# Softmax exponentials without a bias operand: the common factor moved into VectorE's exponent constant

## The chip, the cores and the metric

The kernel runs on one core of a Trainium2 chip. The metric is the device time of one execution in microseconds; lower is better. Every timed kernel was run four times (one of them profiled), next to runs of the kernel before on the same chip; the last experiment was run once.

## The reference, cut to what matters

```python
xn = layernorm(A_x)                                  # [1, 2048, 512]
out = A_x + attention(xn, wqkv, wo) + token_mlp(xn, w1, b1, w2, b2)

def attention(x, wqkv, wo):                          # 32 heads of 16
    q, k, v = split(x @ wqkv)
    p = softmax(q @ k.T * 16 ** -0.5, axis=-1)       # 32 x 2048 x 2048 exponentials
    return merge_heads(p @ v) @ wo
# [the MLP: layernorm, w1 + b1, gelu (tanh form), w2 + b2]
```

There are 134 million exponentials, and the softmax divides by their sum. A factor common to all exponentials of one row therefore cancels; it only has to be the same in numerator and denominator.

## The kernel before

The attention goes through 32 blocks of 32 score tiles. A tile is 128 keys by 1024 columns and fills two PSUM banks; three such slots take turns (`n % 3`). Of the 32 tiles of a block (all blocks but the first), 26 go to ScalarE's `Exp` and six to VectorE, which builds an exponential from integer operations on the bits of a bfloat16: `W` is a first guess, `A` its power of two, `M` a product that corrects the mantissa; TensorE adds up the three.

```python
KAPPA = 2.16705
LNKAPPA = 0.773366911
CM = 171.0 / 1024.0
IBIAS = 16256.0                      # 127 * 128: the exponent bias of bfloat16
DPOS = (2, 7, 12, 17, 22, 27)        # the VectorE tiles of a block of 32
LAG, LAGD = 2, 4                     # periods from scores to the matmuls with V
# ...
kap = sb("kap", [128, 1], F32)
sc.add("pool", lambda e: e.memset(kap[:], LNKAPPA), writes=[("kap",)])
# ...
def pslot(n):
    return n % 2 if n < 2 * NKT else n % 3

def exp_act(n):
    # [buffer bookkeeping cut]
    sc.add("act", lambda e: e.activation(pT[:, buf, :], ps[:, s_ * 1024:(s_ + 1) * 1024], ACTF.Exp,
                                         bias=kap[:], scale=LN2_128),
           reads=[("bank", 2 * s_), ("bank", 2 * s_ + 1), ("kap",)], writes=[("pT", buf)], name="exp")

def exp_dve(n):
    # [buffer bookkeeping cut]
    sc.add("dve", lambda e: e.tensor_scalar(dW_i[:, buf, :], ps[:, s_ * 1024:(s_ + 1) * 1024], IBIAS, 0.0,
                                            ALU.add, ALU.max), ...)              # frees the PSUM slot
    sc.add("dve", lambda e: e.tensor_scalar(dm1_i[:], dW_i[:, buf, :], 0x7f, 0x3f80,
                                            ALU.bitwise_and, ALU.bitwise_or), ...)
    yield                                                                        # next period
    sc.add("dve", lambda e: e.tensor_scalar(dA_i[:, buf, :], dW_i[:, buf, :], -128, None, ALU.bitwise_and), ...)
    sc.add("dve", lambda e: e.tensor_tensor(dm1[:], dm1[:], dm1[:], ALU.mult), ...)
    yield                                                                        # next period
    sc.add("dve", lambda e: e.tensor_tensor(dM[:, buf, :], dW[:, buf, :], dm1[:], ALU.mult), ...)

# the order of the matmuls with V, in pv_seq:
steps.append([g + LAG, [(n, "P") for n in ns]])          # ScalarE tiles
steps.append([g + LAGD, [(n, "W")]])                     # VectorE tiles: three pairs of matmuls
steps.append([g + LAGD, [(n, "A")]])
steps.append([g + LAGD, [(n, "M")]])
```

VectorE's three terms add up to KAPPA times the exponential. So that ScalarE's tiles carry the same factor, their exponentials get the bias ln(KAPPA), which is a pointer to a column of 128 values. A period is one group of two score tiles; TensorE's program runs period by period: the scores of a period, then matmuls with V of earlier periods, then a piece of projections or of the MLP.

The softmax here doesn't subtract the row's maximum and nothing guards it: scores larger than these inputs give would overflow.

## Time and profile before

| | before |
|---|---|
| time, median of 3 (lowest to highest) | 948.09 us (945.67 to 950.41) |
| ScalarE busy | 868.3 us, 91% |
| TensorE busy | 806.3 us, 85% |
| VectorE busy | 778.2 us, 82% |

The engines' busy times, from the first part of the page (engine, busy us, share of the span, instructions):

```profile
PE 806.3 (85%) x5752; PEld 237.4 (25%) x5828; DVE 778.2 (82%) x1296; ACT 868.3 (91%) x859; POOL 35.5 (4%) x78
```

Groups of instructions, from the page (line, engine, operation, output and inputs, shape, count | busy us, mean ns of one | idle us of the engine before them, and what ended most of it):

```profile
L828 ACT ACTIVATE pT<-ps,kap 128x1024 bf16<-128x1024 f32 x838 | 857.6, 1138 | 57.9 <-PE ps L805 55.1
L805 PE MATMUL ps<-QT,KT 32*128 32x512 bf16 x2048 | 328.6, 409 | 104.7 <-ACT pT L828 69.1
L837 DVE TENSOR_SCALAR dW<-ps 128x1024 int16<-128x1024 f32 x186 | 227.0, 1221 | 106.7 <-PE ps L805 105.4
```

838 instructions of 1138 ns would be 954 us, but they are busy for only 857.6: neighbours overlap. So the duration of one is not what it costs. What it costs is the distance from one start to the next when nothing else holds the engine up. ScalarE's timeline shows it (start us, length us, engine, line, operation, count):

```profile
193.83 2.14 ACT L828 ACTIVATE pT<-ps,kap 128x1024 bf16<-128x1024 f32 x2
195.82 0.66 ACT L669 ACTIVATE ga_sb<-ga_sb 128x512 f32<-128x512 f32 x1
196.34 3.16 ACT L828 ACTIVATE pT<-ps,kap 128x1024 bf16<-128x1024 f32 x3
```

Two exponentials take from 193.83 to 195.82, about 996 ns each; the Tanh of the GELU behind them takes 0.52 us until the next start.

Three waits (waits view; who waited for what: us in total, times, longest):

```profile
PE ps L805 <- ACT pT L828: 69.1, 168, 1.6
ACT pT L828 <- PE ps L805: 55.1, 85, 2.2
PE ps L805 <- DVE dW L837: 29.4, 42, 2.7
```

The chain that ended last, by engine and by line:

```profile
ACT 43%; PE 34%; DVE 20%; issue 2%; DMA 1%; SPq 0%; ACTq 0%; POOL 0%; DVEq 0%
```

### The profile page before, as it was taken

How to read it: one execution, taken by the hardware profiler on the slowest of the kernel's cores; microseconds unless marked ns; L12 is line 12 of the kernel's file. 1: busy time of each engine (PE TensorE's matmuls, PEld its weight loads, DVE VectorE, ACT ScalarE, POOL GpSimd, SP SyncE). 2: the span in 40 equal slices, each digit the busy share in tenths (PEclk: the TensorE clock that was granted, in tenths of full speed). 3: DMA queues.
4: the chain of work that ended last, by engine and by line, in shares of the span. 5: the costliest groups of instructions: out<-in, count | busy, mean ns of one | idle time of the engine just before them, and what ended most of it. 6: DMA issues, size and time to landing. Idle time of an engine off the chain costs nothing.

```text
span 949.7 us, 14370 instructions
## 1 busy us (share of the span) xinstructions
PE 806.3 (85%) x5752; PEld 237.4 (25%) x5828; DVE 778.2 (82%) x1296; ACT 868.3 (91%) x859; POOL 35.5 (4%) x78
## 2 busy tenths in 40 slices
PE   5888898988788888888889888998988889788885
PEld 3423233322222222222222222222222222222221
DVE  6688989877788878788888888887888778787787
ACT  5998999998889989899999899998999999999995
POOL 5402000000000000000000000000000000000000
PEclk9989999987888989799999999998999889878898
DMA  5020000011111111111110111100100000000000
GB/s 156 1 51 5 27 6 8 8 29 24 28 29 29 29 23 30 23 21 31 23 42 24 22 37 37 26 20 22 37 22 7 7 7 18 12 7 8 7 8 22
DMA packets 71411, 23.08 MB, mean 24 GB/s; under 512 B 63216, under 2 KB 69360, under 8 KB 71344
## 3 DMA queue, kind: packets, MB, share of 16 engines
q1 hardware_dynamic: 68176, 20.59, 9.8%
q10 hardware_dynamic: 3168, 1.57, 0.6%
q8 instruction: 45, 0.74, 0.3%
q14 instruction: 22, 0.18, 0.1%
HBM read 19.54 MB, written 2.35 MB: 23 GB/s over the span
## 4 chain that ended last, share of the span: by engine, by line
ACT 43%; PE 34%; DVE 20%; issue 2%; DMA 1%; SPq 0%; ACTq 0%; POOL 0%; DVEq 0%
ACT pT L828 42%; PE ps L853 15%; PE ps L805 11%; DVE dW L837 7%; PE ps L654 3%; PE ps L681 2%; DVE dM L849 2%; DVE dm L846 1%; DVE QT L479 1%; DVE dm L840 1%; PE ps L466 1%; DVE KT L456 1%; PE ps L618 1%; DVE u_sb L659 1%; DVE ga_sb L662 1%
## 5 line engine op out<-in xcount | busy, mean ns | idle before, releaser
L828 ACT ACTIVATE pT<-ps,kap 128x1024 bf16<-128x1024 f32 x838 | 857.6, 1138 | 57.9 <-PE ps L805 55.1
L805 PE MATMUL ps<-QT,KT 32*128 32x512 bf16 x2048 | 328.6, 409 | 104.7 <-ACT pT L828 69.1
L837 DVE TENSOR_SCALAR dW<-ps 128x1024 int16<-128x1024 f32 x186 | 227.0, 1221 | 106.7 <-PE ps L805 105.4
L853 PE MATMUL ps<-pT,V 128*32 128x512 bf16 x1676 | 255.8, 416 | 5.8 <-DVE OT L738 4.3
L805 PEld LDWEIGHTS ps<-QT,KT 32*128 32x128 bf16 x2048 | 80.5, 91 | 391.6 <-ACT pT L828 235.3
L849 DVE TENSOR_TENSOR dM<-dW,dm 128x1024 bf16<-128x1024 bf16 x186 | 128.0, 688 | 4.2
L846 DVE TENSOR_TENSOR dm<-dm 128x1024 bf16<-128x1024 bf16 x186 | 127.2, 684 | 0.0
L853 PEld LDWEIGHTS ps<-pT,V 128*32 128x32 bf16 x1676 | 62.6, 97 | 115.8 <-issue 82.1
L840 DVE TENSOR_SCALAR dm<-dW 128x1024 int16<-128x1024 int16 x186 | 80.4, 432 | 6.4
L853 PE MATMUL ps<-dM,VM 128*32 128x512 bf16 x372 | 79.0, 421 | 0.0
L853 PE MATMUL ps<-dW,V 128*32 128x512 bf16 x372 | 78.6, 419 | 0.0
L853 PE MATMUL ps<-dA,V 128*32 128x512 bf16 x372 | 78.2, 417 | 0.0
L844 DVE TENSOR_SCALAR dA<-dW 128x1024 int16<-128x1024 int16 x186 | 76.2, 410 | 0.0
L654 PE MATMUL ps<-big,w1blk 128*128 128x512 bf16 (+1 forms) x156 | 53.0, 413 | 4.0 <-issue 4.0
L681 PE MATMUL ps<-gT,w1blk 128*128 128x512 bf16 (+1 forms) x157 | 51.4, 391 | 3.0 <-issue 3.0
L701 PE MATMUL ps<-wo_pad,oT 128*128 128x512 bf16 x105 | 32.9, 383 | 2.4 <-issue 2.4
L853 PEld LDWEIGHTS ps<-dW,V 128*32 128x32 bf16 x372 | 18.1, 94 | 46.4 <-issue 46.4
L853 PEld LDWEIGHTS ps<-dM,VM 128*32 128x32 bf16 x372 | 20.2, 105 | 25.1 <-issue 6.4
L738 DVE COPY OT<-ps 128x512 f32<-128x512 f32 x31 | 21.3, 688 | 5.7 <-PE ps L853 4.1
L479 DVE TENSOR_SCALAR QT<-ps,qmask 128x512 bf16<-128x512 f32 x30 | 21.1, 744 | 5.3 <-PE ps L466 5.2
L760 DVE TENSOR_TENSOR oT<-OT,denb 128x512 bf16<-128x512 f32 x31 | 21.2, 684 | 0.0
L456 DVE CAST KT<-ps 128x128 bf16<-128x128 f32 (+1 forms) x26 | 12.3, 472 | 9.5 <-PE ps L430 6.3
(74 smaller groups left out, 324.8 us busy)
## 6 DMA issues: line engine op xcount, KB each, us to landing
w1blk<-in_B_w_dram SPq DMA_DIRECT2D x10, 512.0 KB, 4.2
w1blk<-in_B_w_dram SPq DMA_DIRECT2D x16, 320.0 KB, 3.3
denb<-rden_scratch SPq DMA_DIRECT2D x124, 32.0 KB, 1.8
out_dram<-osb SPq DMA_DIRECT2D x16, 128.0 KB, 1.7
dcomp<-OT SPq DMA_DIRECT2D x124, 2.0 KB, 1.7
x_sb<-in_A_x_dram SPq DMA_DIRECT2D x3, 512.0 KB, 9.4
wqkv_sb<-in_A_wqkv_dram ACTq DMA_DIRECT2D x3, 384.0 KB, 11.0
wo_pad<-in_A_wo_dram SPq DMA_DIRECT2D x8, 64.0 KB, 2.0
```

What stands on the lines that cost most here:

```text
L479: sc.add("dve", lambda e, e_=e_, slot=slot: e.tensor_scalar(QT[:, slot, :], bank(bk), qmask[:, e_:e_ + 1], None, ALU.mult), reads=[("bank" ...
L654: sc.add("pe", lambda e, st=st: e.matmul(bank(EX_BANK)[0:m, :], lhsT=w1blk[:, slot, st, 0:m], rhs=h_sb[:, st, :], start=(st == 0), stop=(s ...
L681: sc.add("pe", lambda e, ft=ft, m=m: e.matmul(bank(EX_BANK), lhsT=w2blk[0:m, slot, ft, :], rhs=gT[0:m, ft, :], start=(ft == 0), stop=(ft = ...
L701: sc.add("pe", lambda e, G=G: e.matmul(bank(EX_BANK), lhsT=oT[:, par, G, 128 * sti:128 * (sti + 1)], rhs=wo_pad[:, G, :], start=(G == 0), ...
L805: sc.add("pe", lambda e, r=r, bk=bk: e.matmul(bank(bk), lhsT=KT[32 * r:32 * r + 32, T, 128 * kt:128 * (kt + 1)], rhs=QT[32 * r:32 * r + 32 ...
L828: sc.add("act", lambda e: e.activation(pT[:, buf, :], ps[:, s_ * 1024:(s_ + 1) * 1024], ACTF.Exp, bias=kap[:], scale=LN2_128), reads=[("ba ...
L837: sc.add("dve", lambda e: e.tensor_scalar(dW_i[:, buf, :], ps[:, s_ * 1024:(s_ + 1) * 1024], IBIAS, 0.0, ALU.add, ALU.max), reads=[("bank" ...
L840: sc.add("dve", lambda e: e.tensor_scalar(dm1_i[:], dW_i[:, buf, :], 0x7f, 0x3f80, ALU.bitwise_and, ALU.bitwise_or), reads=[("dW", buf)], ...
L844: sc.add("dve", lambda e: e.tensor_scalar(dA_i[:, buf, :], dW_i[:, buf, :], -128, None, ALU.bitwise_and), reads=[("dW", buf)], writes=[("d ...
L846: sc.add("dve", lambda e: e.tensor_tensor(dm1[:], dm1[:], dm1[:], ALU.mult), reads=[("dm1",)], writes=[("dm1",)], name="dm2")
L849: sc.add("dve", lambda e: e.tensor_tensor(dM[:, buf, :], dW[:, buf, :], dm1[:], ALU.mult), reads=[("dW", buf), ("dm1",)], writes=[("dM", b ...
L853: sc.add("pe", lambda e: e.matmul(bank(PV_BANK)[32 * r:32 * r + 32, :], lhsT=lhs, rhs=rhs, start=first, stop=last, tile_position=(0, 32 * r)),
```

## The change

Instead of bringing ScalarE's exponentials up to KAPPA, VectorE's are brought down: its exponent constant becomes 127·128 − 128·log2(KAPPA), a number that is not an integer. The factor is gone from all tiles, and ScalarE's bias falls back to an immediate zero.

```diff
-LNKAPPA = 0.773366911
-CM = 171.0 / 1024.0
-IBIAS = 16256.0
+IBIAS = 127.0 * 128.0 - 128.0 * float(np.log2(KAPPA))      # CM only moves up
@@
-        kap = sb("kap", [128, 1], F32)
@@
-        sc.add("pool", lambda e: e.memset(kap[:], LNKAPPA), writes=[("kap",)])
@@ exp_act
-                                                 bias=kap[:], scale=LN2_128),
-                   reads=[("bank", 2 * s_), ("bank", 2 * s_ + 1), ("kap",)], writes=[("pT", buf)], name="exp")
+                                                 scale=LN2_128),
+                   reads=[("bank", 2 * s_), ("bank", 2 * s_ + 1)], writes=[("pT", buf)], name="exp")
```

More of the change, by code (lines that the diff above doesn't have):

```diff
@@ L36 @@
 LN2_128 = 0.6931471805599453 / 128.0
+CM = 171.0 / 1024.0
 KAPPA = 2.16705
-LNKAPPA = 0.773366911
-CM = 171.0 / 1024.0
-IBIAS = 16256.0
+IBIAS = 127.0 * 128.0 - 128.0 * float(np.log2(KAPPA))
 DPOS = (2, 7, 12, 17, 22, 27)
```

## The prediction

> **What bounds the kernel now.** Chiefly ScalarE's softmax exponentials. The page's engine table has ScalarE busy 868 us of the 949.7 us span (91%), TensorE 806 (85%), VectorE 778 (82%). The groups table has 838 exponentials of 128x1024 occupying 857.6 us, with only 57.9 us idle before them, nearly all waiting for the score matmuls. The chain of waits runs 42% through them. No engine is far behind: over the 32 blocks of attention ScalarE needs about 27 us a block, VectorE about 25, TensorE about 25, and a block lasts about 28.8 us ((937 - 15)/32, from the timeline). VectorE's share is 186 tiles of 1221 + 432 + 410 + 684 + 688 = 3435 ns (groups), 20 us a block, plus about 4 us of other work.
>
> **What the change does.** The order of instructions is the same on every engine, apart from one small memset at the start that goes away on GpSimd. VectorE's and TensorE's instructions stay the same in number and shape; one VectorE constant is no longer an integer. The only cost that can change is ScalarE's: the 838 exponentials lose their per-partition bias operand; the built program then carries an immediate zero.
>
> **What that is worth each.** From the timeline: back to back, exponentials start every 996 ns, though one lasts 1113 ns or more (they overlap). 1024 elements at the 0.833 ns of the Trainium skill ("ScalarE: Activation LUTs", section "What ACT_TABLE_LOAD costs") are 853 ns, so 143 ns of a period are fixed. The same section says that a pointer operand adds about 93 ns to one activation; the trace agrees: at 512 elements the query copy with a scale pointer took 687 ns, the transposed copies without one 597. But part of this is overlapped. Where the Tanh (no pointer, 512 elements = 427 ns) was issued back to back, the next started 519 ns after it: 92 ns fixed. So I expect the period to fall by about 51 ns, 996 to 945, not by 93; the duration of one should fall by about 90, 1138 to about 1045.
>
> **On the critical path.** 838 x 51 ns = 43 us of ScalarE work. About 82% of ScalarE's instructions start back to back; there the gain counts in full at first. But VectorE, at 25 us a block, then is as long as ScalarE (about 25), and TensorE close behind, also with throttled stretches (granted clock 0.81 from 200 to 300 us, where ScalarE is busy only 84%). Score matmuls already wait 29 us for VectorE's evictions of score tiles (waits view); these waits should grow. I count on 55 to 70% of the 43 us: about 26 us.
>
> **Prediction: 922 us, range 907 to 936 (8 in 10). Faster by over 2% 0.72, within 2% 0.27, slower 0.01.**
>
> **What would show the steps.** (1) Mean duration of an exponential about 1045 ns; spacing back to back about 945 ns in the timeline. (2) ScalarE busy about 825 us. (3) VectorE and TensorE busy within 10 us of 778 and 806, so higher shares. (4) ScalarE's idle time before exponentials up from 58 us by 10 to 25 us, with score matmuls waiting longer for VectorE's evictions and less for ScalarE. (5) The result stays correct.
>
> **What would make it wrong.** The pointer's cost may be wholly hidden in the overlap of neighbours: then the period stays 996 and the time about 948. It may be not hidden at all: period near 905, ScalarE gains 76 us, and the time falls to 895 to 910 with VectorE and TensorE as limits. Exponentials read PSUM and the Tanh SBUF, so the 92 ns may not carry over. [...]

## The result, and the profile after

The changed kernel took 907.27 us (median of 4, 901.64 to 911.73) against 948.39 us (median of 4). The ratio is 0.9565, with a 95% interval of 0.9494 to 0.9636. Here and below, a ratio is the mean time of one kernel's fast runs over that of the other's of the same rounds, so it is not quite the ratio of the medians quoted. The result is correct.

The engines' busy times, and the groups, from the page of after:

```profile
PE 790.7 (87%) x5828; PEld 232.9 (26%) x5828; DVE 775.4 (85%) x1296; ACT 801.4 (88%) x859; POOL 35.5 (4%) x77
```

```profile
L825 ACT ACTIVATE pT<-ps 128x1024 bf16<-128x1024 f32 x838 | 790.6, 1045 | 82.8 <-PE ps L802 79.5
L802 PE MATMUL ps<-QT,KT 32*128 32x512 bf16 x2048 | 312.9, 403 | 91.6 <-ACT pT L825 44.2
L834 DVE TENSOR_SCALAR dW<-ps 128x1024 int16<-128x1024 f32 x186 | 227.1, 1221 | 77.8 <-PE ps L802 77.5
```

The duration of an exponential fell from 1138 to 1045 ns, by 93. VectorE's eviction is unchanged at 1221 ns. TensorE's busy time reads 16 us lower although its instructions are the same (76 matmul records are missing from the trace of before, so that the true fall is larger); its mean granted clock was 0.942 after and 0.920 before. No experiment tells why.

ScalarE's timeline, again around a Tanh behind exponentials:

```profile
189.66 1.98 ACT L825 ACTIVATE pT<-ps 128x1024 bf16<-128x1024 f32 x2
191.46 0.68 ACT L666 ACTIVATE ga_sb<-ga_sb 128x512 f32<-128x512 f32 x1
191.98 5.66 ACT L825 ACTIVATE pT<-ps 128x1024 bf16<-128x1024 f32 x6
```

Two exponentials now take from 189.66 to 191.46: by the starts in the trace 903 ns each, 93 less than the 996 of before. The Tanh, which never had a pointer, still takes 0.52 us.

The waits and the chain:

```profile
ACT pT L825 <- PE ps L802: 79.5, 150, 2.3
PE ps L802 <- ACT pT L825: 44.2, 134, 1.8
PE ps L802 <- DVE dW L834: 40.8, 53, 3.0
```

```profile
PE 42%; DVE 29%; ACT 24%; DMA 2%; issue 2%; SPq 1%; DVEq 0%; ACTq 0%; POOL 0%
```

So the whole saving on ScalarE is 838 × 93 ns = 78 us, but the time fell by 41. To see where the rest went, I call *lost time* the sum of all distances between the starts of neighbouring activations in excess of the back-to-back period, after each exponential: 82.9 us before, 121.2 us after, worked out from the start times in the traces. It rose by 38 us: 78 − 38 = 40 us, which is about what the time gained. So half of what ScalarE saves it loses again between exponentials. Of the 38 us, 24.9 are recorded idle time, nearly all of it ended by score matmuls; most of the rest is lost overlap, because an activation that has to wait does not overlap its predecessor. That happened 197 times in after and 135 times in before; 62 more times at 1045 − 903 = 142 ns make about 9 us, an estimate.

What such a wait looks like, from the timeline of after, all engines:

```profile
703.30 1.22 DVE L834 TENSOR_SCALAR dW<-ps 128x1024 int16<-128x1024 f32 x1
...
704.58 0.39 PE L802 MATMUL ps<-QT,KT 32*128 32x512 bf16 x2 [0.86 <-DVE dW L834]
...
704.89 0.56 PE L850 MATMUL ps<-dW,V 128*32 128x512 bf16 x2
...
704.91 0.58 PE L850 MATMUL ps<-pT,V 128*32 128x512 bf16 x2
...
705.24 0.64 PE L850 MATMUL ps<-dA,V 128*32 128x512 bf16 x2
...
705.67 0.64 PE L850 MATMUL ps<-dM,VM 128*32 128x512 bf16 x2
...
706.67 0.61 PE L802 MATMUL ps<-QT,KT 32*128 32x512 bf16 x4
...
707.32 1.02 ACT L825 ACTIVATE pT<-ps 128x1024 bf16<-128x1024 f32 x1 [1.29 <-PE ps L802]
```

The score matmuls at 704.58 need the slot that VectorE is evicting and wait for it. Behind them, in program order, come the matmuls of an older VectorE tile; only then, at 706.67, the next scores. ScalarE has by then used up its tiles and stands for 1.29 us. Whether it is the eviction, the matmuls or VectorE's total load that counts is a matter for experiments.

One thing makes this example worse than most: the granted TensorE clock was 1.00 from 699.0 to 704.8 us and 0.54 from 704.8 to 708.5 us (windows view), so the matmuls with V in it last 0.56 to 0.64 us instead of the 0.38 to 0.40 of the microseconds before. Such stretches at half clock are a rival explanation of the waits; the traces can settle how much they hold, and the second table of the experiments shows it.

### The profile page after: what moved, and what is told of

Read it like the earlier page. It is cut to its first block, busy times and chain, and to the rows that moved or that the text cites. A ratio compares the mean times of both kernels' runs of the same rounds, so it can differ in the third digit from the quotient of the medians.

```text
span 909.9 us, 14445 instructions
## 1 busy us (share of the span) xinstructions
PE 790.7 (87%) x5828; PEld 232.9 (26%) x5828; DVE 775.4 (85%) x1296; ACT 801.4 (88%) x859; POOL 35.5 (4%) x77
## 4 chain that ended last, share of the span: by engine, by line
PE 42%; DVE 29%; ACT 24%; DMA 2%; issue 2%; SPq 1%; DVEq 0%; ACTq 0%; POOL 0%
ACT pT L825 24%; PE ps L850 18%; PE ps L802 13%; DVE dW L834 11%; PE ps L651 4%; DVE dM L846 3%; PE ps L678 3%; DVE dm L843 2%; PE ps L698 2%; DVE dm L837 2%; DVE QT L476 2%; DVE dA L841 1%; DMA dcomp<-OT 1%; PE ps L615 1%; PE ps L463 1%
## 5 line engine op out<-in xcount | busy, mean ns | idle before, releaser
L825 ACT ACTIVATE pT<-ps 128x1024 bf16<-128x1024 f32 x838 | 790.6, 1045 | 82.8 <-PE ps L802 79.5
L802 PE MATMUL ps<-QT,KT 32*128 32x512 bf16 x2048 | 312.9, 403 | 91.6 <-ACT pT L825 44.2
L834 DVE TENSOR_SCALAR dW<-ps 128x1024 int16<-128x1024 f32 x186 | 227.1, 1221 | 77.8 <-PE ps L802 77.5
L850 PE MATMUL ps<-pT,V 128*32 128x512 bf16 x1676 | 250.4, 408 | 7.6 <-DVE OT L735 6.3
L802 PEld LDWEIGHTS ps<-QT,KT 32*128 32x128 bf16 x2048 | 77.5, 91 | 364.1 <-ACT pT L825 205.3
L850 PE MATMUL ps<-dM,VM 128*32 128x512 bf16 x372 | 76.5, 408 | 0.0
L850 PE MATMUL ps<-dW,V 128*32 128x512 bf16 x372 | 76.4, 407 | 0.0
L850 PE MATMUL ps<-dA,V 128*32 128x512 bf16 x372 | 75.8, 404 | 0.0
L651 PE MATMUL ps<-big,w1blk 128*128 128x512 bf16 (+1 forms) x176 | 56.8, 406 | 0.0
L678 PE MATMUL ps<-gT,w1blk 128*128 128x512 bf16 (+1 forms) x176 | 55.1, 388 | 0.5 <-DVE QT L476 0.5
L698 PE MATMUL ps<-wo_pad,oT 128*128 128x512 bf16 x120 | 36.3, 384 | 0.0
## 6 DMA issues: line engine op xcount, KB each, us to landing
out_dram<-osb SPq DMA_DIRECT2D x16, 128.0 KB, 1.7
```

The costliest lines, as they stand in the source:

```text
L651: sc.add("pe", lambda e, st=st: e.matmul(bank(EX_BANK)[0:m, :], lhsT=w1blk[:, slot, st, 0:m], rhs=h_sb[:, st, :], start=(st == 0), stop=(s ...
L678: sc.add("pe", lambda e, ft=ft, m=m: e.matmul(bank(EX_BANK), lhsT=w2blk[0:m, slot, ft, :], rhs=gT[0:m, ft, :], start=(ft == 0), stop=(ft = ...
L698: sc.add("pe", lambda e, G=G: e.matmul(bank(EX_BANK), lhsT=oT[:, par, G, 128 * sti:128 * (sti + 1)], rhs=wo_pad[:, G, :], start=(G == 0), ...
L802: sc.add("pe", lambda e, r=r, bk=bk: e.matmul(bank(bk), lhsT=KT[32 * r:32 * r + 32, T, 128 * kt:128 * (kt + 1)], rhs=QT[32 * r:32 * r + 32 ...
L850: sc.add("pe", lambda e: e.matmul(bank(PV_BANK)[32 * r:32 * r + 32, :], lhsT=lhs, rhs=rhs, start=first, stop=last, tile_position=(0, 32 * r)),
```

## The experiments

Theory: the pointer operand alone explains what ScalarE gained, and the part that the time did not gain went into waits behind VectorE's score tiles. Rivals: the changed constants matter; TensorE's load or order holds ScalarE up; VectorE's total work does. A lower granted clock is one more; no run was made for it, but the traces bear on it.

| run | median us | ratio to before (95% interval) | period, ns | lost time, us |
|---|---|---|---|---|
| before | 948.39 | 1 | 996 | 82.9 |
| after | 907.27 | 0.9565 (0.9494 to 0.9636) | 903 | 121.2 |
| e1_zero_pointer | 948.15 | 0.9988 (0.9926 to 1.0051) | 996 | 79.6 |
| e2_two_pointers | 997.96 | 1.0491 (1.0391 to 1.0590) | 1090 | 49.7 |
| e3_less_vector | 892.37 | 0.9407 (0.9348 to 0.9466) | 904 | 103.8 |
| e4_less_tensor | 897.88 | 0.9458 (0.9397 to 0.9519) | 904 | 101.8 |
| e5_five_after | 950.80 | 1.0060 (0.9995 to 1.0124) | 903 | 126.1 |
| e6_five_before | 979.81 | 1.0330 (1.0271 to 1.0390) | 996 | 79.3 |
| e7_short_eviction | 864.93 | 0.9126 (0.9074 to 0.9178) | 904 | 74.1 |
| e11_spread_terms | 889.01 | 0.9379 (0.9327 to 0.9432) | 903 | 99.8 |
| e13_evict_first | 916.43 | 0.9621 (0.9558 to 0.9685) | 904 | 125.9 |
| e14_evict_spread | 898.10 | 0.9449 (0.9421 to 0.9478) | 904 | 106.9 |
| e15_five_other | 907.11 | 0.9542 (0.9481 to 0.9603) | 904 | 81.3 |

Periods are medians of the distances between back-to-back exponentials, and lost time is worked out as above. The runs come from three chips, each beside seven runs of before (medians 947.32 to 949.63 us); so runs are compared by their ratios.

The same lost time, divided by the granted TensorE clock. It is worked out from the start times and the clock record of each profiled run; an interval counts as half clock when more than half of it lies in a stretch that was granted 0.5.

| run | time at half clock, us | lost time there, us | lost time at full clock, us |
|---|---|---|---|
| before | 152 | 45 | 38 |
| after | 106 | 37 | 84 |
| e3_less_vector | 99 | 31 | 73 |
| e4_less_tensor | 123 | 41 | 61 |
| e5_five_after | 168 | 65 | 61 |
| e7_short_eviction | 72 | 22 | 52 |
| e11_spread_terms | 151 | 46 | 53 |
| e15_five_other | 116 | 30 | 51 |

The loss that the change added lies at full clock, 38 to 84 us: the throttle did not cause it. But about a third of what is lost in after falls into the 106 us at half clock. How long a run stays at half clock differs between the kernels, and no run explains it, so the lost time at full clock is the fairer measure of a change in waits.

### e1_zero_pointer: the pointer back, pointing at zeros

```diff
+        kap = sb("kap", [128, 2], F32)
+        sc.add("pool", lambda e: e.memset(kap[:, 0:1], 0.0), writes=[("kap",)])
@@ exp_act of after
-                                                 scale=LN2_128),
+                                                 bias=kap[:, 0:1], scale=LN2_128),   # and ("kap",) read
```

> The changed kernel with the pointer put back but pointing at zeros: the arithmetic of after, the operand form of before. Theory (the pointer operand alone is what changed the time): exponentials last about 1138 ns on average, start every 996 ns back to back, and the time is that of before, 944 to 952 us. Rival (the value of the bias or VectorE's non-integer constant matters): the time stays nearer to 907 us, below 930. The result must be correct.

Measured: 948.15 us, correct, period 996 ns, mean duration 1141 ns. From its page:

```profile
L827 ACT ACTIVATE pT<-ps,kap 128x1024 bf16<-128x1024 f32 x838 | 857.4, 1141 | 54.8 <-PE ps L804 51.8
```

The arithmetic is that of after and the time that of before, within 0.7% either way. What changed the time is the form of the operand; VectorE's non-integer constant costs nothing that shows.

### e2_two_pointers: the cost doubled

```diff
@@ exp_act of after, kap as above, kap[:, 1:2] filled with LN2_128
-                                                 scale=LN2_128),
+                                                 bias=kap[:, 0:1], scale=kap[:, 1:2]),
```

> Both bias (zeros) and scale (the same constant in every partition) as pointers: the suspected cost doubled. Theory (each pointer adds about 93 ns to the period, none of it hidden; and the more ScalarE binds, the more of it shows in the time): period about 1089 ns, ScalarE's exponentials +78 us over before, the time up by 60 to 78 us over before, 1005 to 1028 us, against 41 us for the step from none to one. Rival (fetches of two pointers overlap each other): period 996 to 1040 and a time below 985 us.

Measured: correct, period 1090 ns, median 997.96 us (one of the four runs was slow at 1008.33 us and is not in the ratio). The group of exponentials on its page:

```profile
L828 ACT ACTIVATE pT<-ps,kap 128x1024 bf16<-128x1024 f32 x838 | 929.0, 1248 | 35.1 <-PE ps L805 32.1
```

The period does as the theory says: 903, 996, 1090 for none, one and two pointers. The time does so less than expected: by the ratio +47 us on before (37 to 56), not 60 to 78. So steps of equal size on ScalarE, 78 us each, are worth about 47 us from two pointers to one and 41 us (35 to 48) from one to none; the intervals overlap, so the times do not show that the first step is worth more. The lost time does grow from step to step: 50, 83, 121 us. Even with two pointers ScalarE was not the only limit; the return was already partial at before.

### e3_less_vector: 127 us of VectorE's work gone

```diff
@@ exp_dve of after (wrong result on purpose)
-            sc.add("dve", lambda e: e.tensor_tensor(dm1[:], dm1[:], dm1[:], ALU.mult),
-                   reads=[("dm1",)], writes=[("dm1",)], name="dm2")
```

> The changed kernel without the squaring of the mantissa on VectorE: wrong result on purpose, 186 x 685 ns = 127 us of VectorE's work gone, TensorE's and ScalarE's as in after. Theory (the unused 37 us of the 78 us went into waits for VectorE, which evicts its score tiles late in its queue): ScalarE's idle time before exponentials falls from 83 to 45 to 60 us and the time to 870 to 890 us. Rival (TensorE's order and its 87% busy share hold ScalarE up): under 8 us gained, above 899 us.

Measured: 892.37 us (wrong result), lost time 104 us. The gain of 15 us lies between the two expectations: less than the theory's 17 to 37, more than the rival's 8. Taking away a sixth of VectorE's work returns only a part of the loss (at full clock, 84 to 73 us). VectorE's total is not the main matter.

### e4_less_tensor: the matmuls with the exponent tiles gone

```diff
@@ pv_seq of after (wrong result on purpose)
-                        steps.append([g + LAGD, [(n, "A")]])
```

> The changed kernel without the 372 matmuls on the exponent tiles dA: wrong result on purpose, about 186 x 2 x 0.21 = 40 us (at most 76 us by busy time) of TensorE's work gone, all in the periods with a VectorE tile. VectorE's and ScalarE's work as in after. Theory (waits for VectorE): 0 to 12 us gained, above 895 us. Rival (TensorE): 20 us or more gained, below 887 us, and ScalarE's idle time down to 60 us or less.

Measured: 897.88 us, lost time 102 us. The gain of about 10 us is within the theory's 0 to 12, but its interval overlaps that of after, so it is not clear. The rival's 20 us or more did not come in the time. But this run stood longer at half clock than after (123 against 106 us); at full clock its lost time fell from 84 to 61 us, more than in e3. So these matmuls do hold ScalarE up, as e11 shows from another side.

### e7_short_eviction: VectorE sets the slot free earlier

```diff
@@ exp_dve of after (wrong result on purpose; dW cleared once at the start)
-            sc.add("dve", lambda e: e.tensor_scalar(dW_i[:, buf, :], ps[:, s_ * 1024:(s_ + 1) * 1024], IBIAS, 0.0,
+            sc.add("dve", lambda e: e.tensor_scalar(dW_i[:, buf, 0:512], ps[:, s_ * 1024:s_ * 1024 + 512], IBIAS, 0.0,
```

> The changed kernel with VectorE evicting only half of each of its score tiles (the other half stays stale, wrong result on purpose): the eviction takes about 0.67 instead of 1.22 us, 186 x 0.55 = 102 us of VectorE's work gone, less than in the run without the squaring (127 us, which won 15 us). Theory (what counts is how late VectorE sets its score tile free, as the in-order score matmuls behind it need that slot): at least twice that gain, 868 to 880 us. Rival (VectorE's total work counts): about 12 us gained, 890 to 900 us.

Measured: 864.93 us (wrong result), below the expected 868 to 880; lost time 74 us. From its page and its waits view:

```profile
L826 ACT ACTIVATE pT<-ps 128x1024 bf16<-128x1024 f32 x838 | 783.5, 1056 | 44.9 <-PE ps L803 41.2
L835 DVE TENSOR_SCALAR dW<-ps 128x512 int16<-128x512 f32 x186 | 128.0, 688 | 100.1 <-PE ps L803 99.6
```

```profile
PE ps L803 <- DVE dW L835: 16.5, 16, 2.0
```

VectorE lost 99 us of work (227.1 to 128.0), less than the 127 of e3, yet the gain on after is 42 us instead of 15. Score matmuls wait 16.5 us for evictions instead of 40.8, and ScalarE's lost time falls below that of before. So a microsecond of VectorE's work counts about 3.6 times as much in the eviction, where it holds a PSUM slot, as in the squaring, where it holds none (42/99 against 15/127). e7 also stood less at half clock (72 us, against 99 in e3 and 106 in after), but that does not make the difference: at full clock alone the lost time fell by 32 us in e7 and by 11 in e3, again some 3.7 times as much for a microsecond of work.

### e11_spread_terms: the same matmuls, not in one burst

```diff
@@ pv_seq of after
-                        steps.append([g + LAGD, [(n, "W")]])
-                        steps.append([g + LAGD, [(n, "A")]])
+                        steps.append([g + LAGD - 2, [(n, "W")]])
+                        steps.append([g + LAGD - 1, [(n, "A")]])
```

> The changed kernel with the three pairs of matmuls of a VectorE tile in three successive periods instead of all in one (no work added or taken, correct result). Theory (bursts of TensorE's in-order work delay the next score matmuls and so ScalarE): 8 to 20 us gained, 887 to 900 us, ScalarE's idle time down accordingly. Rival (only sums of work and the eviction count): within 5 us of 907.

Measured: 889.01 us, correct, as the theory expected. ScalarE's idle time before exponentials fell from 82.8 to 60.8 us:

```profile
L825 ACT ACTIVATE pT<-ps 128x1024 bf16<-128x1024 f32 x838 | 791.3, 1042 | 60.8 <-PE ps L802 54.6
```

Not one instruction was added or taken; the matmuls of a VectorE tile only stand in three periods instead of one. So TensorE's order, with the same matmuls, takes a share of the loss. Its busy time still reads 20 us lower (771.0 instead of 790.7), so whether the new order shortens the work itself or only the wait behind it is not separated. This is the fastest correct kernel, at 0.9379 of before; its interval does not touch that of after. It did so at a lower granted clock than after (0.915 against 0.942 in the profiled runs); at full clock its lost time fell from 84 to 53 us.

### e13_evict_first and e14_evict_spread: the eviction issued earlier

```diff
@@ exp_dve of after: a yield between the eviction and the mask
                    reads=[("bank", 2 * s_), ("bank", 2 * s_ + 1)], writes=[("dW", buf)], name="dexp")
+            yield
@@ main loop: first the new tile's eviction, then the older tile's product
-            for ch in d_next:
-                if next(ch, True) is None:
-                    d_chain.append(ch)
+            new_d = []
 ...
-                        d_chain.append(ch)
+                        new_d.append(ch)
 ...
+            for ch in d_next + new_d:
+                if next(ch, True) is None:
+                    d_chain.append(ch)
```

> The changed kernel with VectorE's order altered in three of the six tiles of a block: the eviction of a new score tile is issued ahead of the last product of the tile before it, instead of behind it (0.69 us earlier in the queue); same instructions, correct result. Theory (the lateness of the eviction counts): 6 to 26 us gained on the changed kernel's 907, 881 to 901 us. Rival (VectorE has nothing to do there anyway until the scores come, so order is of no use): within 4 us of 907.

> The run with the three pairs of matmuls spread over three periods (889 us) together with the earlier eviction: if the two act on different waits they add: 866 to 884 us, faster than both kernels of the study. If they act on the same waits: 884 to 892 us. Correct result.

Measured: e13 916.43 us, not faster than after (the intervals overlap), and e14 898.10 us, not faster than e11, which lacks this edit (intervals 0.9421 to 0.9478 and 0.9327 to 0.9432, which just overlap). Both also lie above all that was expected of them (901 us, or level with 907, for e13; 892 for e14). The theory that the eviction's place in the queue counts fell. From the page of e13:

```profile
L834 DVE TENSOR_SCALAR dW<-ps 128x1024 int16<-128x1024 f32 x186 | 227.2, 1221 | 100.9 <-PE ps L802 100.4
```

VectorE stood 100.9 us before evictions instead of 77.8: put ahead, the eviction waits for scores that are not there yet. It probably holds up the product behind it, which no run tests. What e7 shortened is the time that the eviction itself takes; that is not the same as starting it earlier in the program.

### e5_five_after, e6_five_before and e15_five_other: one VectorE tile fewer

```diff
@@ e5 on after, e6 on before
-DPOS = (2, 7, 12, 17, 22, 27)
+DPOS = (2, 8, 14, 20, 26)
@@ e15 on after
-DPOS = (2, 7, 12, 17, 22, 27)
+DPOS = (7, 12, 17, 22, 27)
```

> The changed kernel with five instead of six VectorE tiles in each block of 32: 31 tiles go back to ScalarE, +31 x 903 ns = 28 us there, -31 x 3435 ns = 106 us on VectorE, and 124 matmuls fewer on TensorE. If waits caused by VectorE's tiles (their eviction, their six matmuls) make up ScalarE's 121 us of lost time, a sixth of them goes and the rest shorten: 895 to 912 us, about level with the changed kernel's 907. If ScalarE's own work is what counts: 925 to 935 us.

> The same shift of tiles in the kernel before: +31 x 996 ns = 31 us on ScalarE. Theory (before is nearer to ScalarE's limit, so the shift pays less): 955 to 972 us, a ratio to six tiles higher by at least 1% than for the changed kernel. Rival (the best split did not move): the two ratios are within 0.5% of each other.

> Five VectorE tiles a block again, but the old positions without the first (7, 12, 17, 22, 27), which lies right behind the block change. In the other run with five, VectorE stood 38 us at a reciprocal that waits for a DMA, just ahead of the first tile of a block, and the time was 951 us. Theory (the placing, not the number of tiles, cost the most there): 912 to 932 us, ScalarE's lost time under 110 us. Rival (fewer VectorE tiles cost that much in themselves): 943 us or more.

Measured: e5 took 950.80 us, far above both readings; e6 979.81 us, also above its range; e15 907.11 us, below its range and level with after. e5 and e15 have the same compute instructions in the same numbers, 44 us apart in their medians and 49 by their ratios. So these runs say nothing on the best number of tiles until the placing is right. One difference shows in the page of e5:

```profile
L747 DVE RECIPROCAL rcomp<-dcomp 128x16 f32<-128x16 f32 x31 | 7.8, 252 | 37.7 <-DMA dcomp<-OT 37.7
```

In e5 VectorE stands 37.7 us at a reciprocal that waits for a DMA, 32.7 us in e6, but 3.4 us in after and 3.5 us in e15 (waits views). That could cover some 34 us of the difference, but no run takes this wait away alone; that it is the cause is not shown. Two rivals stand untested. The positions of e5 are six apart, so that within a block all its VectorE tiles take the same one of the three PSUM slots (`n % 3`); those of e15, five apart, take the slots in turn. And e5 was at half clock for 168 us, e15 for 116: of the 45 us of lost time between their traces, 35 fall into these stretches. The expectation that the kernel before would gain less from five tiles than after cannot be judged: the ratio of five to six tiles is 1.033 in before and 1.006/0.9565 = 1.052 in after, with bad placing in both.

### e16_probe: the period by itself

48 activations, six of each kind, stand at the start of the changed kernel, one behind the other, after PSUM and the sources were cleared.

```diff
+        for i in range(6):
+            probe(gT[:, i, :], P512, ACTF.Exp, [("gT", i)], BK, scale=LN)
+        for i in range(6):
+            probe(oT[:, 1, i, :], P512, ACTF.Exp, ..., bias=kap[:, 0:1], scale=LN)
 ... (six more kinds)
```

> The changed kernel with 48 extra activations back to back at the start, six of each kind, to measure the period by itself; the time of the run means nothing, the result is correct. 512 elements are 427 ns. Exp from PSUM to bf16: no pointer 477 ns, bias pointer 570 ns, bias and scale pointers 663 ns (+93 each). The prediction took 92 ns fixed from the Tanh. Theory (that Tanh is dearer because it reads SBUF): Exp from SBUF 519 ns, Tanh from PSUM 477 ns, Tanh from SBUF 519 ns. Rival (the float32 output): Exp from PSUM to float32 519 ns, Exp from SBUF to bf16 477 ns. Rival (the function): both Tanh 519 ns, all Exp without pointer 477 ns. Exp of 1024 from PSUM without pointer: 903 ns.

Its ScalarE timeline (a group of 12 holds two kinds, of six each; dA and dM are one kind):

```profile
7.84 3.05 ACT L570 ACTIVATE gT<-ps 128x512 bf16<-128x512 f32 x6 [1.67 <-DVE ps L563]
10.72 7.64 ACT L570 ACTIVATE oT<-ps,kap 128x512 bf16<-128x512 f32 x12
18.12 3.35 ACT L570 ACTIVATE pT<-u_sb 128x512 bf16<-128x512 f32 x6
21.23 3.16 ACT L570 ACTIVATE big<-ps 128x512 f32<-128x512 f32 x6
24.10 3.40 ACT L570 ACTIVATE big<-u_sb 128x512 f32<-128x512 f32 x6
27.22 5.77 ACT L570 ACTIVATE pT<-ps 128x1024 bf16<-128x1024 f32 x6
32.65 2.29 ACT L570 ACTIVATE dA<-ps 128x512 bf16<-128x512 f32 x4
34.55 1.36 ACT L570 ACTIVATE dM<-ps 128x512 bf16<-128x512 f32 x2
```

The starts of the groups, six apart, give the periods; the single starts in the trace agree:

| activation, 128x512 unless said | period, ns |
|---|---|
| Exp, PSUM to bf16, no pointer | 478 |
| the same, bias pointer | 570 |
| the same, bias and scale pointers | 663 |
| Exp, SBUF to bf16, no pointer | 519 |
| Exp, PSUM to float32, no pointer | 478 |
| Tanh, SBUF to float32, no pointer | 520 |
| Tanh, PSUM to bf16, no pointer | 478 |
| Exp, PSUM to bf16, 128x1024, no pointer | 904 |

Every pointer costs 92 to 93 ns of the period, none of it hidden. Reading from SBUF instead of PSUM costs 42 ns; the function and the output's type cost nothing here. The first theory, of the three on the Tanh, is the right one.

## Why the prediction was right or wrong

The time, 907.27 us, lies within the stated range of 907 to 936 us, at its edge; the call "faster by over 2%" was right. The central value, 922, was 15 us too high. Point by point:

- **ScalarE bounds it and only the operand's form changes: right.** e1 brings the time of before back with a pointer to zeros.
- **The duration falls by about 90 to about 1045 ns: right.** It fell from 1138 to 1045.
- **"I expect the period to fall by about 51 ns, 996 to 945, not by 93": this is the term that was mis-sized.** The period fell by 93, to 903. The prediction took its fixed 92 ns from the Tanh, the only activation without a pointer that ran back to back. But the Tanh reads SBUF and the exponentials read PSUM. The probe shows that an activation that reads SBUF has a period 42 ns longer, which is just the part of the pointer's 93 ns that I took for hidden. The prediction named this danger at its end, as well as a period near 905, and gave both too little weight.
- **ScalarE busy about 825 us:** 801.4, so the forecast was 24 us too high, by the same error. The busy time fell by 67 us and not by 838 × 93 ns = 78, since fewer neighbours overlap.
- **"I count on 55 to 70%": about right, slightly high.** 41 of 78 us arrived, 53%. The two errors have opposite signs, the larger one in the period. So that the time fell into the range was partly luck: 55 to 70% of the true 78 us would have been 43 to 55 us, 894 to 905 us, below the range.
- **VectorE and TensorE within 10 us of their busy time: right for VectorE** (775.4), not for TensorE (790.7, 16 us lower), which no run explains.
- **ScalarE's idle time up by 10 to 25 us:** up by 24.9, from 57.9 to 82.8.
- **Waits shift from ScalarE to VectorE's evictions: right.** Score matmuls waited 40.8 us for evictions (29.4 before) and 44.2 us for ScalarE (69.1). That VectorE, by its total of 25 us a block, is then the limit was the wrong reason: e3 and e7 show that the time for which the eviction holds a slot counts far more than VectorE's total, and e11 that TensorE's order has a share.

What stays open: how the 38 us divide between eviction and order, since e7 and e11 were not run together; why an earlier eviction did not help at all; what makes the two placings of five tiles differ by 44 to 49 us; why the granted clock rose from before to after, and why it differs between the kernels. Spread terms with five tiles at the positions of e15 was not run, and may be faster than e11.

## What to carry to other kernels

In these runs a per-partition pointer on an activation cost its full 93 ns every time, even in a dense stream, so fold constants into something that already takes an immediate. Read an engine's cost from the distance between back-to-back starts, and take it from instructions with the same source memory; a gauge that reads from elsewhere misled here by 42 ns. When the busiest engine is relieved and others are near, expect only a part of the saving (here about half), and look next at who holds the shared buffers and what stands in order behind them: moving the six matmuls of a VectorE tile apart won 18 us at no cost in work.

## What the Trainium skill lacked or had wrong

- "ScalarE: Activation LUTs", section "What ACT_TABLE_LOAD costs": that each pointer operand adds about 93 ns agrees with these runs (period 903, 996, 1090 ns for none, one, two at 1024 elements; 478, 570, 663 at 512). The page does not say in so many words that none of this cost is hidden between back-to-back activations; none is.
- The same section gives 186 ns + 0.833·N and an overlap of about 93 ns, which make 520 ns for 512 elements without pointer. That is right for a source in SBUF (519 and 520 ns measured) and 42 ns too much for one in PSUM (478 ns; at 1024 elements 946 by the page, 903 to 904 measured). This page does not tell the two sources apart, but the skill does not lack it: the page "Perfetto Trace Analysis", section "Optimizing Scalar/DVE Operations", gives ScalarE a fixed overhead for each of the two, and the probe agrees with it (about 92 ns from SBUF and 51 from PSUM, beyond 427 ns for the elements).
- The same section's overlap is not a constant in the records: in the probe, with each instruction issued behind the last, the recorded durations of the 128x1024 exponentials averaged 1222 ns in its groups view and the period stayed at 904. That is an overlap of 318 ns instead of 93, and in the changed kernel it is 142 (1045 − 903). The page does not warn that a mean duration in a profile can exceed the cost by that much; the section named in the point before says that recorded durations exceed the engine's own time, but by less than the probe shows.
